# A spectral layer followed by two feed-forward stages on one core: swapping two halves of a result tile with GpSimd copies in place of four DMAs

## The chip, the cores and the metric

The kernel runs on one core of one Trainium2 chip. The metric is the device time in microseconds (us) from one launch, and the figure for a kernel is the median over its runs.

## The reference

The work is a chain of three layers over `x` of shape (4, 3072, 256), in float32.

```python
X = np.fft.rfft(x, axis=1)                       # layer 1: 3072-point spectrum
Yr = Xr @ w_r - Xi @ w_i + b_r                   # complex 256x256 mix of every frequency
Yi = Xr @ w_i + Xi @ w_r + b_i
Y  = sign(Y) * max(abs(Y) - 0.01, 0)             # soft shrink, real and imaginary part
y  = np.fft.irfft(Y, n=3072, axis=1)
xk, xr = mixes of y and y shifted by one token   # layer 2: 256 -> 1024 -> 256, gated
z  = sigmoid(xr @ w_r) * (max(xk @ w_k, 0)**2 @ w_v)
out = (h * tanh(softplus(h))) @ w_out            # layer 3: h = z @ w_in, 256 -> 2048 -> 256
```

## The kernel before

Most products are made of three matmuls in a reduced float32 format: each operand is split into a high part (a ScalarE copy that rounds) and a low part (a VectorE subtraction), and high x high, high x low and low x high are summed in PSUM. The function `split` does this, so its two lines L77 (ScalarE) and L78 (VectorE) stand for many tiles, and tiles are told apart by name.

The transform is a 96 x 32 factorisation. It takes place in the first fifth of the time. The pieces are:

- `s1(b, q)`, the 96-point stage: 32 calls of 8 products, from tiles `xs`/`XS0` of `x` and the table `FC`. The first 12 calls use plain float32. Tiles carry the 96 rows at partitions 16 to 111, and 16 rows of zeros ahead of them are written by GpSimd (`new_x`) and VectorE (`new_F`), so that products run over 112 rows. `s1_ev` copies results out and stores them to device memory.
- a loop over 48 groups `u` (a turn of the loop below), 12 for each of the four batches. A turn issues `s2(u + 1)`, the 32-point stage from a tile `A` that `load_A` fetched and `split_A` split; `s2_ev(u + 1)`, which splits its result from PSUM into `Xh`, `Xl`; `mix(u)`, the complex mix by three real products with tables `WX` (`k1p` is the shared product, `mxp` the two sums, and the bias enters as a product of `SEL` and `BR`); `above(u)` and `shrink(u)`, the soft shrink; and `is1(u - 2)`, the 32-point inverse stage, from `Yh`, `Yl`, which `split_Y(u - 2)` made. `is1_ev(u - 3)` copies the result out of the one PSUM buffer `i1p` into a tile `Cs`, and stores it. In 20 of the turns (2 to 5, and two of every three from 8 to 30) an `s1` is issued as well; the others are called plain turns below.
- from turn 33 on, `early(k)` begins the 96-point inverse stage and layer 2 within the loop.

The result of `mix` has the real and imaginary halves of one group in the same partitions but in an order that the inverse stage can't use. `shrink(u)` therefore writes its result over the tile `yt` (one buffer), and four DMAs on SP's queue copy quarters of it (64 partitions x 256) into a tile `Y` with the halves rearranged. The next `mix` writes `yt` again, and so has to wait for those DMAs.

Engines run their instructions in the order of the code; nothing is reordered. Small steps of the weight preparation for layers 2 and 3 are put between (`bg(2)`, twice a turn): a weight takes 17 steps, eight of which are VectorE instructions on 128x512 elements. After the loop come layer 2 (L886, L924 and others) and layer 3 (L1140, L1188, L1189).

Of the kernel before, what the change touches and what calls it, by code (L numbers as in the profile page):

```python
# [8 lines left out]
F32 = mybir.dt.float32  # L9
# [4 lines left out]
ALU = mybir.AluOpType  # L14
# [15 lines left out]
def kernel(  # L30
# [129 lines left out]
    ps1p = ps1.__enter__()  # L160

    FC = p1sp.tile([128, N2, 2, N1], F32R, name="FC")
    PAD = 16
    KR, XR = slice(0, PAD + N1), slice(PAD, PAD + N1)
    MC = p1p.tile([128, 2, 2, 192], F32R, name="MC")
    WC = p1p.tile([128, 2, 2, 128], F32R, name="WC")
    WX = p1p.tile([128, 2, 3, 2, D], F32R, name="WX")
# [6 lines left out]
    def new_F(q):  # L174
        tag, n = ((("dec_v", 1), ("dec_b", 1)) + (("Cs", 2),) * 2 + (("A", 4),) * 4)[q]
        Ft[q] = p1p.tile([128, 512], F32, tag=tag, name="ctmp", bufs=n)
        nc.vector.memset(Ft[q][0:PAD, 0:384], 0.0)

    def load_F(q):
        for c in (slice(0, 192), slice(192, 384)) if q == 0 else (slice(0, 384),):  # L180
            nc.sync.dma_start(out=Ft[q][XR, c], in_=c_f[:, q * 384 + c.start:q * 384 + c.stop])
            yield

    def split_F(q):
        v = Ft[q][KR, 0:384].rearrange("p (n c) -> p n c", n=4)
        split(v, FC[KR, 4 * q:4 * q + 4, 0, :], FC[KR, 4 * q:4 * q + 4, 1, :])

    cst = {}

# [40 lines left out]
        split(v, WX[:, :, c, 0, :], WX[:, :, c, 1, :])  # L230

    def load_bias():
        t = cst["b"] = p1p.tile([128, 2, D], F32, tag="T", name="bias", bufs=2)
        nc.gpsimd.memset(t, 0.0)
        for p, n in ((0, 1), (32, 1), (64, 2), (96, 2)):
            for k in range(n):
                nc.sync.dma_start(out=t[p:p + 1, k, :], in_=b_r.partition_broadcast(1))
        for p in (0, 32):
            nc.sync.dma_start(out=t[p:p + 1, 1, :], in_=b_i.partition_broadcast(1))

    def make_bias():
        t = cst["b"]
        nc.scalar.copy(out=BR, in_=t)
        for p in (32, 96):
            nc.vector.tensor_tensor(out=BR[p:p + 1], in0=t[p:p + 1], in1=BR[p:p + 1], op=ALU.subtract)

    def make_sel():
        t = p1p.tile([128, 512], F32, tag="T", name="sel", bufs=2)
        s, z = t[:, 0:256].rearrange("p (k n) -> p k n", k=2), t[:, 256:512]
        nc.gpsimd.memset(t, 0.0)  # L250
        for p in (0, 32):
            nc.gpsimd.memset(s[p:p + 1], 1.0)
            nc.gpsimd.memset(s[p:p + 1, 1, 96:97], 0.0)
# [30 lines left out]

    def new_x(b, q):
        t = xs_t[b, q] = p1sp.tile([128, 4, D], F32, tag="xs", name="xs", bufs=3) if b else XS0[q // 4][:, q % 4]
        nc.gpsimd.memset(t[0:PAD], 0.0)

    def x_loads(b, q):
        xv = x[b].rearrange("(p n) d -> p n d", n=N2)[:, 4 * q:4 * q + 4, :]  # L290
        for c in (slice(0, 2), slice(2, 4)) if b + q == 0 else (slice(0, 4),):
            nc.sync.dma_start(out=xs_t[b, q][XR, c], in_=xv[:, c, :])
            yield

    def load_x(b, q):
        new_x(b, q)
        for _ in x_loads(b, q):
            pass

    def split_x(b, q):  # L300
        t = xs_t.pop((b, q))
        h = p1sp.tile([128, 4, D], F32R, tag="xh", name="xh", bufs=3)
        l = p1sp.tile([128, 4, D], F32R, tag="xl", name="xl", bufs=3)
        split(t[KR], h[KR], l[KR])
        xh_t[b, q] = (h, l)

    def warm(n):
# [8 lines left out]
    def s1(b, q):  # L316
        i = 8 * b + q
        plain = i < NAT
        if plain:
            h = xs_t.pop((b, q))  # L320
            f = Ft[q][:, 0:384].rearrange("p (n c) -> p n c", n=4)
        else:
            h, l = xh_t.pop((b, q))
        if b == 0:
            st = XS0[q // 4][0:N1, q % 4]
        elif i < 11:
            st = pkp.tile([N1, 4, D], F32, tag=("D", "Dh", "Dl")[q], name="st", bufs=1)
        else:
            st = p1sp.tile([N1, 4, D], F32, tag="st", name="st", bufs=2)
        for e in range(2):  # L330
            p = ps1p.tile([N1, 2, D], F32, tag=("s1" if i >= NAT or e == 0 else "mx"), name="s1p")
            for m in range(2):
                n2 = 4 * q + 2 * e + m
                if plain:
                    nc.tensor.matmul(
                        out=p[:, m, :], lhsT=f[KR, 2 * e + m, :], rhs=h[KR, 2 * e + m, :], start=True, stop=True
                    )
                    continue
                for k, (w, v) in enumerate(((0, h), (0, l), (1, h))):
                    nc.tensor.matmul(  # L340
                        out=p[:, m, :], lhsT=FC[KR, n2, w, :], rhs=v[KR, 2 * e + m, :],
                        start=(k == 0), stop=(k == 2),
                    )
            s1_t.append((b, q, e, st, p))

    def s1_ev():
        b, q, e, st, p = s1_t.popleft()
        if e == 1 or 8 * b + q >= NAT:
            nc.scalar.copy(out=st[:, 2 * e:2 * e + 2, :], in_=p)
        else:  # L350
            nc.vector.tensor_copy(out=st[:, 0:2, :], in_=p)
# [11 lines left out]
    def store_kept(q):  # L363
        nc.sync.dma_start(out=scr1[1][:, 4 * q:4 * q + 4, :], in_=kept.pop(q))
# [93 lines left out]

    def shrink(u):
        t, up = mx_t.pop(u)  # L460
        nc.vector.scalar_tensor_tensor(out=t, in0=t, scalar=LAM, in1=up, op0=ALU.add, op1=ALU.min)
        y = Y_t[u] = p1p.tile([128, 2, D], F32, tag="T", name="Y", bufs=2)
        for e in range(2):
            for c in range(2):
                nc.sync.dma_start(out=y[64 * c:64 * c + 64, e, :], in_=t[64 * e:64 * e + 64, c, :])

    def split_Y(u):
        yh = p1p.tile([128, 2, D], F32R, tag="Yh", name="Yh", bufs=2)
# [267 lines left out]
    for u in range(NU + 3):  # L736
        if 0 < u < NU - 1:
            s2(u + 1)
        if s1_t:
            s1_ev()  # L740

        def fill():
            if 2 <= u < NU + 2:
                split_Y(u - 2)
            while s1_t:
                s1_ev()
            if u > 2:
# [36 lines left out]
        if u > U_E:
            early(u - U_E - 1)
# [538 lines left out]
```

## Time and profile before

| | |
|---|---|
| median of 3 runs | 2070.87 us (2067.3 to 2074.36) |
| the profiled execution | 2071.17 us, of which its span is 2069.4 us |
| TensorE busy | 1991.1 us, 96% of the span |
| VectorE busy | 1515.1 us, 73% |
| ScalarE busy | 1172.2 us, 57% |
| GpSimd busy | 57.2 us, 3% |

TensorE's busy time is a mean over stages that differ. Below, a stretch is named by its bounds in us from the span's start. The loop's turns are counted by the VectorE instruction at L451, which makes the sum of `mix`: turn 0's starts at 55.59, turn 1's at 62.28, turn 32's at 283.83 and turn 47's, the last, at 379.49.

### The profile page before, as it was taken

The page shows a single profiled execution, that of the slowest core. Times are in us where ns is not written, and L with a number is a line of the kernel's source. Part 1 is how long each engine was busy: PE and PEld are TensorE (multiplying, and loading weights), DVE is VectorE, ACT ScalarE, POOL GpSimd, SP SyncE. Part 2 cuts the span into 40 slices and gives each one's busy share as a digit, 9 for nine tenths or more (in the row PEclk, how much of TensorE's full clock was granted, in tenths as well). Part 3 has the DMA queues.
Part 4 walks back from the last instruction along what each step waited for, and adds up shares of the span by engine and source line. Part 5 has one row for each costly group of instructions (what it writes and reads, how often), then busy time and mean ns, then how long its engine had stood idle before and what let it go on. Part 6 is the DMA issues. An engine that isn't in the chain of part 4 may idle for free.

```text
span 2069.4 us, 33457 instructions
## 1 busy us (share of the span) xinstructions
PE 1991.1 (96%) x13026; PEld 1886.1 (91%) x13026; DVE 1515.1 (73%) x2451; ACT 1172.2 (57%) x1793; POOL 57.2 (3%) x77
## 2 busy tenths in 40 slices
PE   7888888899999999999999999999999999999999
PEld 5777777799999999999989999999999999999998
DVE  5677777577777677777558877778777877778785
ACT  3566655677777777777654444444444444444444
POOL 3100000000000000000000000000000000000000
PEclk8999989899999999999999999999999999999999
DMA  8676755321212121212010000100010100100000
GB/s 258 175 199 195 203 154 143 92 65 49 75 47 75 49 65 57 67 58 65 16 46 22 30 23 21 32 24 29 21 32 21 30 23 21 32 24 29 22 11 21
DMA packets 87117, 135.64 MB, mean 66 GB/s; under 512 B 9448, under 2 KB 63952, under 8 KB 86960
## 3 DMA queue, kind: packets, MB, share of 16 engines
q1 hardware_dynamic: 83376, 120.93, 20.4%
q0 software_dynamic: 3584, 12.58, 1.6%
q8 instruction: 103, 1.69, 0.4%
q14 instruction: 54, 0.44, 0.1%
HBM read 70.56 MB, written 50.33 MB: 58 GB/s over the span
## 4 chain that ended last, share of the span: by engine, by line
PE 81%; ACT 0%; DVE 0%; issue 0%; ACTq 0%
PE h L1140 19%; PE o L1188 17%; PE kp L886 13%; PE vp L924 13%; PE o L1189 9%; PE pp L863 3%; PE p L1140 3%; PE pp L562 3%; PE hp L829 1%; PE h0p L829 0%; PE i1p L480 0%; PE s1p L562 0%; PE pp L536 0%; ACT Yh L77 0%; ACT Cs L492 0%; DVE ob L1204 0%
## 5 line engine op out<-in xcount | busy, mean ns | idle before, releaser
L1188 PE MATMUL o<-WO,gh 128*128 128x512 f32 x1536 | 562.0, 394 | 0.0
L1189 PE MATMUL o<-WO,gl 128*128 128x256 f32 x1536 | 430.3, 280 | 0.0
L1140 PE MATMUL h<-xS,WS 128*128 128x256 f32 x2208 | 350.9, 281 | 0.0
L1153 ACT COPY p1s<-p 128x256 f32<-128x256 f32 x184 | 68.5, 372 | 471.9 <-PE p L1140 470.9
L1188 PEld LDWEIGHTS o<-WO,gh 128*128 128x128 f32 x1536 | 288.9, 188 | 43.3
L1140 PEld LDWEIGHTS h<-xS,WS 128*128 128x128 f32 x2208 | 299.6, 188 | 16.1
L886 PE MATMUL kp<-xk,WK 128*128 128x384 f32 x1536 | 292.2, 338 | 0.0
L1189 PEld LDWEIGHTS o<-WO,gl 128*128 128x128 f32 x1536 | 289.5, 188 | 0.2
L924 PE MATMUL vp<-kh,WV 128*128 128x384 f32 x1024 | 281.2, 336 | 0.0
L886 PEld LDWEIGHTS kp<-xk,WK 128*128 128x128 f32 x1536 | 268.9, 189 | 0.3
L1143 DVE TENSOR_TENSOR C<-h,p1s 128x512 f32<-128x512 f32 x184 | 127.2, 691 | 158.3 <-PE h L1140 156.3
L911 DVE TENSOR_TENSOR kl<-kr,kh 128x768 fp32r<-128x768 f32 x128 | 122.9, 960 | 162.3 <-ACT kr L910 160.9
L1125 DVE TENSOR_TENSOR gl<-g,gh 128x1024 fp32r<-128x1024 f32 x184 | 223.7, 1216 | 2.1 <-ACT g L1122 2.1
L1121 ACT ACTIVATE gh<-C 128x1024 fp32r<-128x1024 f32 x184 | 195.7, 1064 | 10.8 <-DVE C L1143 10.7
L1122 ACT ACTIVATE g<-C 128x1024 f32<-128x1024 f32 x184 | 193.1, 1050 | 0.0
L1140 PE MATMUL h<-xS,WI 128*128 128x256 f32 x1104 | 189.8, 280 | 0.0
L1143 DVE TENSOR_TENSOR C<-h,wu 128x512 f32<-128x512 f32 x368 | 187.7, 552 | 0.3 <-PE h L1140 0.3
L924 PEld LDWEIGHTS vp<-kh,WV 128*128 128x128 f32 x1024 | 186.2, 188 | 0.0
L924 PE MATMUL vp<-kl,WV 128*128 128x384 f32 x512 | 171.5, 335 | 0.0
L909 ACT ACTIVATE kh<-kr 128x768 fp32r<-128x768 f32 x128 | 108.3, 846 | 89.3 <-PE vp L924 89.1
L1140 PEld LDWEIGHTS h<-xS,WI 128*128 128x128 f32 x1104 | 155.7, 188 | 0.0
L1143 DVE TENSOR_TENSOR wu<-h,C 128x512 f32<-128x512 f32 x184 | 126.6, 688 | 34.9 <-PE h L1140 31.1
(187 smaller groups left out, 3143.1 us busy)
## 6 DMA issues: line engine op xcount, KB each, us to landing
Y<-yt SPq DMA_DIRECT2D x192, 64.0 KB
scr<-Cs SPq DMA_DIRECT2D x48, 256.0 KB
D<-scr SPq DMA_DIRECT2D x32, 384.0 KB
x2d<-r POOLq DMA_DIRECT2D x32, 384.0 KB, 3.5
x<-x2d SPq DMA_DIRECT2D x24, 512.0 KB
out_dram<-ob SPq DMA_DIRECT2D x96, 128.0 KB
A<-scr SPq DMA_DIRECT2D x44, 256.0 KB
xs<-in_x_dram SPq DMA_DIRECT2D x24, 384.0 KB
```

The lines of the kernel that those rows point to most:

```text
L886: nc.tensor.matmul(out=p[:, m, 0:TA], lhsT=WK[:, dh, w, f * 128:(f + 1) * 128], rhs=hl[:, v, dh, :], start=(i == 0), stop=(i == 5),)
L909: nc.scalar.activation(out=kh, in_=kr, func=AF.Square)
L911: nc.vector.tensor_tensor(out=kl, in0=kr, in1=kh, op=ALU.subtract)
L924: nc.tensor.matmul(out=p[:, o, 0:TA], lhsT=WV[:, f, w, o * 128:(o + 1) * 128], rhs=v[:, m, :], start=(f == 0 and i == 0), stop=(f == 7 and ...
L1121: nc.scalar.activation(out=gh, in_=c, func=AF.Mish)
L1122: nc.scalar.activation(out=g, in_=c, func=AF.Mish)
L1125: nc.vector.tensor_tensor(out=gl, in0=g, in1=gh, op=ALU.subtract)
L1140: nc.tensor.matmul(out=out, lhsT=a(l), rhs=xS[:, v, b, :], start=(n == 0), stop=(n == 2))
L1143: nc.vector.tensor_tensor(out=out, in0=x0, in1=x1, op=ALU.add)
L1153: nc.scalar.copy(out=p1s, in_=p1)
L1188: nc.tensor.matmul(out=o[m], lhsT=gh[:, m2, ms], rhs=WO[:, f], start=(f == 0), stop=False)
L1189: nc.tensor.matmul(out=o[m][:, 0, :], lhsT=gl[:, m2, ms], rhs=WO[:, f, 0, :], start=False, stop=(f == 15))
```

## The change

Five things change. The shrink writes straight into `Y`, and three GpSimd copies of 64 x 256 rearrange it in place, through a small tile `sw` that takes its place in the one-buffer ring `K1`, which the ScalarE copy `K` of `mix` uses too. `split_A` stands a turn later. `is1_ev` stands at the head of a turn rather than behind `split_A`. Zero rows are gone: tiles hold 96 rows at partitions 0 to 95. Ahead of the loop, the mix tables and the bias are loaded and prepared sooner, and the bias is spread over the rows that need it by GpSimd copies instead of six DMAs.

```diff
     def load_bias():
-        t = cst["b"] = p1p.tile([128, 2, D], F32, tag="T", name="bias", bufs=2)
+        t = cst["b"] = p1p.tile([128, 2, D], F32, tag="Yl", name="bias", bufs=2)
         nc.gpsimd.memset(t, 0.0)
-        for p, n in ((0, 1), (32, 1), (64, 2), (96, 2)):
-            for k in range(n):
-                nc.sync.dma_start(out=t[p:p + 1, k, :], in_=b_r.partition_broadcast(1))
-        for p in (0, 32):
-            nc.sync.dma_start(out=t[p:p + 1, 1, :], in_=b_i.partition_broadcast(1))
+        nc.sync.dma_start(out=t[0:1, 0, :], in_=b_r.partition_broadcast(1))
+        nc.sync.dma_start(out=t[0:1, 1, :], in_=b_i.partition_broadcast(1))
 
     def make_bias():
         t = cst["b"]
+        nc.gpsimd.tensor_copy(out=t[32:33], in_=t[0:1])
+        for p in (64, 96):
+            for k in range(2):
+                nc.gpsimd.tensor_copy(out=t[p:p + 1, k, :], in_=t[0:1, 0, :])
         nc.scalar.copy(out=BR, in_=t)
         for p in (32, 96):
-            nc.vector.tensor_tensor(out=BR[p:p + 1], in0=t[p:p + 1], in1=BR[p:p + 1], op=ALU.subtract)
+            nc.gpsimd.tensor_tensor(out=BR[p:p + 1], in0=t[p:p + 1], in1=BR[p:p + 1], op=ALU.subtract)
...
     def new_x(b, q):
         t = xs_t[b, q] = p1sp.tile([128, 4, D], F32, tag="xs", name="xs", bufs=3) if b else XS0[q // 4][:, q % 4]
-        nc.gpsimd.memset(t[0:PAD], 0.0)
...
     def shrink(u):
         t, up = mx_t.pop(u)
-        nc.vector.scalar_tensor_tensor(out=t, in0=t, scalar=LAM, in1=up, op0=ALU.add, op1=ALU.min)
         y = Y_t[u] = p1p.tile([128, 2, D], F32, tag="T", name="Y", bufs=2)
-        for e in range(2):
-            for c in range(2):
-                nc.sync.dma_start(out=y[64 * c:64 * c + 64, e, :], in_=t[64 * e:64 * e + 64, c, :])
+        nc.vector.scalar_tensor_tensor(out=y, in0=t, scalar=LAM, in1=up, op0=ALU.add, op1=ALU.min)
+        w = p1p.tile([128, D], F32, tag="K1", name="sw", bufs=1)[0:64]
+        nc.gpsimd.tensor_copy(out=w, in_=y[64:128, 0, :])
+        nc.gpsimd.tensor_copy(out=y[64:128, 0, :], in_=y[0:64, 1, :])
+        nc.gpsimd.tensor_copy(out=y[0:64, 1, :], in_=w)
...
+    load_consts()
+    load_bias()
+    load_A(2)
     load_x(1, 3)
-    load_A(2)
     s1(1, 2)
...
     s2(0)
-    s1(1, 3)
+    split_mix(0)
     s2_ev(0)
     split_A(1)
+    split_mix(2)
+    split_mix(1)
+    make_bias()
+    s1(1, 3)
...
     s2_ev(1)
-    split_mix(0)
-    make_bias()
-    split_mix(2)
-    split_mix(1)
     load_A(4)
...
     for u in range(NU + 3):
         if 0 < u < NU - 1:
             s2(u + 1)
+        if u > 2:
+            is1_ev(u - 3)
         if s1_t:
             s1_ev()
...
-        if u + 4 < NU:
-            split_A(u + 4)
-        if u > 2:
-            is1_ev(u - 3)
+        if 0 < u < NU - 3:
+            split_A(u + 3)
```

The order of the instructions on an engine shows what this moves. First ScalarE (ACT) in the loop, from turn 10's `K` to turn 11's, as it was; `K` is the copy of the shared product, `yc` belongs to the shrink, and a name in brackets is the engine or DMA whose semaphore the instruction waits for.

```order
L449 COPY K_1294<-k1p 128x256 [waits PE_49,Activation_49]
L456 ACTIVATE yc<-yt 128x512 [waits DVE_49]
L77 CAST Xh<-s2p 128x768 [waits PE_49]
L77 CAST Yh<-Y 128x512 [waits DMAHW4_49,DMAHW5_49,DMAHW3_49,DMAHW2_49]
L77 CAST Ah<-A 128x512 [waits DMAHW7_49]
L492 COPY Cs<-i1p 128x512 [waits DMAHW0_49]
L449 COPY K_1365<-k1p 128x256 [waits PE_49,Activation_49]
```

And the same stretch of the changed kernel.

```order
L446 COPY K_1260<-k1p 128x256 [waits PE_49,Activation_49,Pool_49]
L453 ACTIVATE yc<-yt 128x512 [waits DVE_49]
L490 COPY Cs<-i1p 128x512 [waits DMAHW4_49,PE_49]
L77 CAST Xh<-s2p 128x768 [waits PE_49]
L77 CAST Yh<-Y 128x512
L77 CAST Ah<-A 128x512 [waits DMAHW6_49]
L446 COPY K_1331<-k1p 128x256 [waits PE_49,Activation_49,Pool_49]
```

`Cs` has moved from fifth place behind `yc` to the first, `Yh` waits for no DMA any more, and `K` has a new wait for GpSimd (Pool). On GpSimd itself the loop before holds only the zero rows (one instruction in each turn with an `s1`); now these are the rows of two turns.

```order
L461 COPY sw<-Y 64x256 [waits DVE_49]
L462 COPY Y<-Y 64x256 [waits Pool_49]
L463 COPY Y<-sw 64x256 [waits Pool_49]
L461 COPY sw<-Y 64x256 [waits DVE_49]
L462 COPY Y<-Y 64x256 [waits Pool_49]
L463 COPY Y<-sw 64x256 [waits Pool_49]
```

The three copies run one after another, each waiting for the one ahead. The third place is the DMA queue of SP ahead of the loop, before the change: `yt` and `yc` are the buffers that the mix weights are loaded into, and `A`, `xs`, `st` and `XS` are the tiles named above.

```order
L378 DMA A<-scr1a 128x2x256 x2
L292 DMA xs<-in_x_dram 96x1024
L378 DMA A<-scr1a 128x2x256
L367 DMA scr_0_57<-XS_82 64x1024 x2
L200 DMA yt<-in_w_r_dram 128x2x256
L200 DMA yc<-in_w_i_dram 128x2x256
L292 DMA xs<-in_x_dram 96x1024
L378 DMA A<-scr1a 128x2x256
L237 DMA bias<-in_b_r_dram 1x256 x6
L239 DMA bias<-in_b_i_dram 1x256 x2
L364 DMA scr_1_58<-st 96x1024
```

And with the change.

```order
L375 DMA A<-scr1a 128x2x256 x2
L197 DMA yt<-in_w_r_dram 128x2x256
L197 DMA yc<-in_w_i_dram 128x2x256
L232 DMA bias<-in_b_r_dram 1x256
L233 DMA bias<-in_b_i_dram 1x256
L375 DMA A<-scr1a 128x2x256
L289 DMA xs<-in_x_dram 96x1024
L364 DMA scr_0_57<-XS_82 64x1024 x2
L289 DMA xs<-in_x_dram 96x1024
L375 DMA A<-scr1a 128x2x256
L361 DMA scr_1_58<-st 96x1024
```

The weights and the bias have moved ahead of one `A` and one `xs` load, and six DMAs are gone from in front of the store. TensorE's instructions stand in the same order in both kernels.

## Rows read from the trace of the kernel before

**Rows 1.** Busy time by stretch; the columns name themselves, PEclk is the granted clock

```profile
62.28:283.83 221.55, 182.05 (x1298) 168.59 (x1297) 157.50 (x230) 139.11 (x263) 15.06 (x15) 0.96 0.68 191
283.83:379.49 95.66, 78.43 (x539) 71.62 (x537) 68.53 (x113) 52.31 (x105) 0.00 (x0) 0.94 0.53 143
379.49:389.22 9.73, 4.75 (x14) 3.99 (x15) 5.49 (x17) 4.38 (x13) 0.00 (x0) 0.54 0.31 89
389.22:2069.40 1680.18, 1676.13 (x10981) 1604.19 (x10979) 1251.86 (x2036) 951.96 (x1367) 24.58 (x33) 1.00 0.12 38
```

**Rows 2.** Waits from 62.28 to 389.22: who waited for whom, total, times, longest

```profile
PE i1p L480 <- ACT Cs L492: 55.5, 32, 5.2
DVE yt L451 <- DMA Y<-yt: 50.0, 37, 4.6
...
ACT Ah L77 <- DMA A<-scr: 10.8, 10, 2.8
```

**Rows 3.** Timeline of turn 43, a plain turn: start, duration, instruction, wait

```profile
355.19 0.69 DVE L451 TENSOR_TENSOR yt<-mxp,K 128x512 f32<-128x512 f32 x1 [1.01 <-DMA Y<-yt]
...
356.58 0.69 DVE L461 SCALAR_TENSOR_TENSOR yt<-yt,yc 128x512 f32<-128x512 f32 x1 [0.70 <-ACT yc L456]
...
357.30 2.38 SPq L465 DMA_DIRECT2D Y<-yt  x4
...
359.81 0.37 ACT L449 COPY K<-k1p 128x256 f32<-128x256 f32 x1
...
361.22 0.69 DVE L451 TENSOR_TENSOR yt<-mxp,K 128x512 f32<-128x512 f32 x1 [0.28 <-DMA Y<-yt]
```

**Rows 4.** TensorE's timeline at full clock: parts of two turns with an s1

```profile
63.28 0.28 PE L340 MATMUL s1p<-xh,FC 112*96 112x256 f32 x1
...
64.58 0.28 PE L340 MATMUL s1p<-xh,FC 112*96 112x256 f32 x1
...
72.96 0.50 PE L480 MATMUL i1p<-Yh,WC 128*128 128x512 f32 x1
...
73.76 0.36 PE L396 MATMUL s2p<-MC,Ah 128*128 128x192 f32 x2
...
77.48 0.28 PE L340 MATMUL s1p<-xh,FC 112*96 112x256 f32 x1
```

**Rows 5.** VectorE's groups from 62.28 to 283.83: busy us, mean ns, idle before

```profile
L78 DVE TENSOR_TENSOR xl<-xs,xh 112x1024 fp32r<-112x1024 f32 x18 | 21.9, 1216 | 0.0
...
L137 DVE SCALAR_TENSOR_TENSOR dec_v<-dec_b,dec_v 128x512 f32<-128x512 int32 x7 | 4.9, 693 | 0.2
...
L126 DVE TENSOR_SCALAR dec_b<-dec_v 128x512 int32<-128x512 int32 x7 | 3.0, 427 | 0.2
```

**Rows 6.** GpSimd's groups of the whole span, by shape

```profile
L78 POOL TENSOR_TENSOR x2h<-x,x2h 128x1024 fp32r<-128x1024 f32 x1 | 2.4, 2396 | 9.8 <-PE vp L924 9.8
L252 POOL MEMSET sel<- 1x256 f32 x2 | 0.6, 304 | 0.1
```

**Rows 7.** Timeline late in layer 2: GpSimd's one subtraction and VectorE beside it

```profile
1027.26 0.96 DVE L911 TENSOR_TENSOR kl<-kr,kh 128x768 fp32r<-128x768 f32 x1 [0.66 <-ACT kr L910]
...
1031.07 1.19 DVE L911 TENSOR_TENSOR kl<-kr,kh 128x768 fp32r<-128x768 f32 x1 [2.25 <-ACT kr L910]
...
1029.05 2.40 POOL L78 TENSOR_TENSOR x2h<-x,x2h 128x1024 fp32r<-128x1024 f32 x1 [9.79 <-PE vp L924]
```

**Rows 8.** Timeline ahead of the loop: SP's queue, ScalarE, VectorE

```profile
35.99 4.80 SPq L237 DMA_DIRECT2D bias<-in_b_r_dram  x6
...
48.09 2.85 SPq L378 DMA_DIRECT2D A<-scr  x2
...
54.33 0.62 ACT L77 CAST Ah<-A 128x512 fp32r<-128x512 f32 x1 [3.07 <-DMA A<-scr]
...
55.59 0.68 DVE L451 TENSOR_TENSOR yt<-mxp,K 128x512 f32<-128x512 f32 x1
```

**Rows 9.** TensorE's timeline behind the last turn

```profile
383.01 0.80 PE L480 MATMUL i1p<-Yh,WC 128*128 128x512 f32 x1 [5.20 <-ACT Cs L492]
```

More of the change, by code (lines that the diff above doesn't have):

```diff
@@ L162 @@
     FC = p1sp.tile([128, N2, 2, N1], F32R, name="FC")
-    PAD = 16
-    KR, XR = slice(0, PAD + N1), slice(PAD, PAD + N1)
     MC = p1p.tile([128, 2, 2, 192], F32R, name="MC")
@@ L176, in new_F @@
         Ft[q] = p1p.tile([128, 512], F32, tag=tag, name="ctmp", bufs=n)
-        nc.vector.memset(Ft[q][0:PAD, 0:384], 0.0)
     def load_F(q):
         for c in (slice(0, 192), slice(192, 384)) if q == 0 else (slice(0, 384),):
-            nc.sync.dma_start(out=Ft[q][XR, c], in_=c_f[:, q * 384 + c.start:q * 384 + c.stop])
+            nc.sync.dma_start(out=Ft[q][0:N1, c], in_=c_f[:, q * 384 + c.start:q * 384 + c.stop])
             yield
     def split_F(q):
-        v = Ft[q][KR, 0:384].rearrange("p (n c) -> p n c", n=4)
-        split(v, FC[KR, 4 * q:4 * q + 4, 0, :], FC[KR, 4 * q:4 * q + 4, 1, :])
+        v = Ft[q][0:N1, 0:384].rearrange("p (n c) -> p n c", n=4)
+        split(v, FC[0:N1, 4 * q:4 * q + 4, 0, :], FC[0:N1, 4 * q:4 * q + 4, 1, :])
     cst = {}
@@ L232, in load_bias @@
     def load_bias():
-        t = cst["b"] = p1p.tile([128, 2, D], F32, tag="T", name="bias", bufs=2)
+        t = cst["b"] = p1p.tile([128, 2, D], F32, tag="Yl", name="bias", bufs=2)
         nc.gpsimd.memset(t, 0.0)
-        for p, n in ((0, 1), (32, 1), (64, 2), (96, 2)):
-            for k in range(n):
-                nc.sync.dma_start(out=t[p:p + 1, k, :], in_=b_r.partition_broadcast(1))
-        for p in (0, 32):
-            nc.sync.dma_start(out=t[p:p + 1, 1, :], in_=b_i.partition_broadcast(1))
+        nc.sync.dma_start(out=t[0:1, 0, :], in_=b_r.partition_broadcast(1))
+        nc.sync.dma_start(out=t[0:1, 1, :], in_=b_i.partition_broadcast(1))
     def make_bias():
         t = cst["b"]
+        nc.gpsimd.tensor_copy(out=t[32:33], in_=t[0:1])
+        for p in (64, 96):
+            for k in range(2):
+                nc.gpsimd.tensor_copy(out=t[p:p + 1, k, :], in_=t[0:1, 0, :])
         nc.scalar.copy(out=BR, in_=t)
         for p in (32, 96):
-            nc.vector.tensor_tensor(out=BR[p:p + 1], in0=t[p:p + 1], in1=BR[p:p + 1], op=ALU.subtract)
+            nc.gpsimd.tensor_tensor(out=BR[p:p + 1], in0=t[p:p + 1], in1=BR[p:p + 1], op=ALU.subtract)
     def make_sel():
-        t = p1p.tile([128, 512], F32, tag="T", name="sel", bufs=2)
+        t = p1p.tile([128, 512], F32, tag="Yh", name="sel", bufs=2)
         s, z = t[:, 0:256].rearrange("p (k n) -> p k n", k=2), t[:, 256:512]
@@ L291, in x_loads @@
         for c in (slice(0, 2), slice(2, 4)) if b + q == 0 else (slice(0, 4),):
-            nc.sync.dma_start(out=xs_t[b, q][XR, c], in_=xv[:, c, :])
+            nc.sync.dma_start(out=xs_t[b, q][0:N1, c], in_=xv[:, c, :])
             yield
@@ L303, in split_x @@
         l = p1sp.tile([128, 4, D], F32R, tag="xl", name="xl", bufs=3)
-        split(t[KR], h[KR], l[KR])
+        split(t[0:N1], h[0:N1], l[0:N1])
         xh_t[b, q] = (h, l)
@@ L335, in s1 @@
                     nc.tensor.matmul(
-                        out=p[:, m, :], lhsT=f[KR, 2 * e + m, :], rhs=h[KR, 2 * e + m, :], start=True, stop=True
+                        out=p[:, m, :], lhsT=f[0:N1, 2 * e + m, :], rhs=h[0:N1, 2 * e + m, :], start=True, stop=True
                     )
@@ L340, in s1 @@
                     nc.tensor.matmul(
-                        out=p[:, m, :], lhsT=FC[KR, n2, w, :], rhs=v[KR, 2 * e + m, :],
+                        out=p[:, m, :], lhsT=FC[0:N1, n2, w, :], rhs=v[0:N1, 2 * e + m, :],
                         start=(k == 0), stop=(k == 2),
@@ L645 @@
     store_rest(5)
-    load_consts()
     load_x(1, 4)
     load_A(3)
-    load_bias()
     make_sel()
     s2(0)
-    s1(1, 3)
+    split_mix(0)
     s2_ev(0)
     split_A(1)
+    split_mix(2)
+    split_mix(1)
+    make_bias()
+    s1(1, 3)
     store_kept(0)
```

## The prediction

> **What bounds the kernel now.** I read the table of busy time by stretch first. From 389.22 us to the end TensorE is busy for 1676.13 of 1680.18 us at a granted clock of 1.00 [rows 1]. The change touches nothing there, and no wait taken from another engine could shorten it. All that can move lies in the first 389 us, which is the start up to turn 0, the loop and its tail. In the two stretches of the loop TensorE is busy for 182.05 of 221.55 us and 78.43 of 95.66 us, VectorE for 157.50 and 68.53, and the granted clock averages 0.96 and 0.94 [rows 1], so some of TensorE's busy time is at 1.2 GHz instead of 2.4. No engine is full here; a chain of waits sets the pace.
>
> The list of waits names it. TensorE waits 55.5 us in front of the inverse stage for `Cs`, the copy that empties its one PSUM buffer, and VectorE waits 50.0 us, in 37 of 47 turns, for the DMAs that read `yt` [rows 2]. The timeline of a plain turn shows how these are one chain. The sum `yt` starts at 355.19, the shrink ends at 357.27, four DMAs are then issued over 2.38 us, and the next `yt` starts at 361.22, let go by the DMA although `K` was ready at 360.18 [rows 3]. So a turn is 6.03 us, of which 3.95 us is the handover through DMA. ScalarE stands in `yc` until `yt` comes, and `Cs` is queued behind it; that is the wait of TensorE.
>
> **The change, part by part.** *Handover.* The four DMAs go, and `yt` is free once the shrink has read it. In place of them the next `K` waits for the third copy. The new chain of a turn is 2.08 us from `yt` to the end of the shrink, three copies of c us with a hop of about 0.06 us each, `K` at 0.37 us [rows 3], and two hops of some 0.05 us: 2.73 + 3c. No copy of GpSimd is in the trace. From below there is its memset of 256 elements, which is 304 ns; from above its subtraction, 2396 ns for 1024 elements or 2.34 ns each, which gives 0.60 us for 256, and 0.70 with a start-up cost [rows 6]. A copy has one input where the subtraction has two, so it is nearer to the memset; I take c = 0.40 us. Turns by this chain are then 3.93 us, and 3.64 to 4.83 at the bounds. That is below what TensorE needs, so the handover stops being the bound and the engines' own work is next.
>
> The Trainium skill ("GPSIMD Engine Reference", section 3.1) has about 1 cycle per element for an operation bound by one port and 2.6 for one with two inputs; as an estimate from that page a copy would be about 0.31 us with the memset's start-up, and the chain 3.7 us.
>
> *TensorE's own work.* At full clock the 32-point stage and the mix take 3.72 us (73.76 to 77.48), the inverse stage 0.80 (72.96 to 73.76), and an `s1` 1.42 (eleven spacings in 63.28 to 64.58, times 12/11) [rows 4]. A plain turn needs 4.52 us and one with an `s1` 5.94. *VectorE's own work.* Its 157.50 us over 31 turns hold 21.9 us of `xl` [rows 1, 5]. A weight costs five instructions of about 0.69 us and three of about 0.42 [rows 5], 4.7 us in 17 steps at four a turn, so 1.1 a turn. Without both, a turn needs 135.6 / 31 - 1.1 = 3.27 us, and one with an `s1` 4.49. The weight's eight instructions fall into about two of every 4.25 turns, which need 2.36 us more: 5.63 plain, 6.85 with an `s1`. In these VectorE is the bound; in the others TensorE is. The mean is 0.47 x 6.85 + 0.53 x 5.94 = 6.37 us with an `s1`, and 0.47 x 5.63 + 0.53 x 4.52 = 5.04 plain.
>
> *GpSimd beside VectorE.* A VectorE subtraction with both operands in SBUF took 1.19 us instead of 0.96 when it started at 1031.07, while GpSimd's subtraction ran until 1031.45 [rows 7]: 0.23 us lost in 0.38 of overlap, or 0.6 of it. The copies start behind the shrink, and take 3 x 0.46 = 1.4 us; the next on VectorE is `Xl`, one of whose operands is in PSUM, for about 0.9 us, and then `Yl` with two in SBUF. If only `Yl` is hit, a turn loses about 0.6 x 0.4 = 0.2 us where VectorE is the bound, 0.1 on average. From below the loss is nothing; from above all 1.4 us of copying is lost in every turn.
>
> The Trainium skill ("SBUF — State Buffer", section "Who interferes with whom") says that a VectorE instruction with two SBUF inputs contends with a GpSimd instruction that reads SBUF, and that the loser is blocked fully rather than slowed. By that rule the loss is the whole overlap, 0.4 us in place of 0.2, which over 46 turns adds some 5 us to the sum; the row has 0.6 of the overlap, so it agrees on the collision but not on its size. It speaks against the change, and is the first rival below.
>
> *Sum of the loop.* Turns 1 to 32: 20 x 6.47 + 11 x 5.14 = 186 us, against 221.55 before [rows 1]: -36. Turns 32 to 47 are plain but carry the first parts of layer 2, some 4 us of TensorE; I take 5.14 + 0.26 = 5.4 us, 81 against 95.66 [rows 1]: -15. The limits from below are TensorE's 168.5 and 72 us.
>
> *`is1_ev` first, `split_A` later.* Moving `Cs` up takes `Xh`, `Yh` and `Ah` from in front of it, which would otherwise still hold TensorE back once the DMA wait is gone. Its own store is the same DMA, now ahead of the store of `st` and the load of `A` on SP's queue; each is one issue of about half a us that no one waits for. `Ah` now waits a turn less early for its load. Of the 10.8 us of waits for `A` and the few for other loads [rows 2] I leave half to come back on a path: +7 us.
>
> *Start.* On SP eight bias issues become two; six took 4.80 us [rows 8]. The loads of `A` behind them, issued at 48.09, held ScalarE until 54.33, and turn 0's sum was at 55.59 [rows 8]. The `Ah` that waited is a turn later now, and the tables are cast while ScalarE waits for the 96-point stage anyway. Against that one `xs` load stands behind 0.5 MB of weights and comes about 2 us later. I take -4 us; the bounds are 0 and -7. *Tail.* TensorE waits 5.20 us for `Cs` at 383.01, behind the last DMA handover [rows 9]; with a handover of 1.4 us instead of 4 and `Cs` at the head, -4 us of the 9.73.
>
> *Zero rows.* 32 GpSimd memsets and eight of VectorE go; GpSimd is busy for 15.06 of 221.55 us [rows 1] and nothing waits for it in the loop. Fewer rows don't shorten a product: 31 of the 32-point stage and the mix, over 128 rows, take 0.120 us each, and those of `s1`, over 112, 0.118 [rows 4]; so 96 rows are 0, and so are the six tiny copies of the bias, hidden behind the wait for the next `A`.
>
> Total: -36 - 15 + 7 - 4 - 4 = -52 us. The profiled execution took 2071.17 us, 0.3 above the median, so 2071 - 52 gives about **2019 us**.
>
> **Rivals.** (1) *Blocked VectorE.* If VectorE loses all 1.4 us of copying, it needs 1.3 more than my sum allows in 46 turns: +60 us, or 2079 at worst and about 2060 where half falls into idle time. `Xl` with its PSUM operand and TensorE's bound in half the turns speak against it. (2) *Another wait behind the first.* Loads of `A`, stores and the k1p and st hand-ons follow closely, and turns shorten by half as much: 2071 - 27 = 2044. The 10.8 us for `A` speaks for it; the DMA share of 0.68 [rows 1], of which the four copies go, against. (3) *Slower: slow copies.* `K` waits for the third copy, and everything on ScalarE behind `K`. The turn is 2.73 + 3c; the loop becomes longer than before when this passes (221.55 + 95.66 + 8) / 46 = 7.07 us, at c = 1.45 us. At c = 1.6 it is 7.53 x 46 - 317 - 8 = +21, or 2092. The copies cross partitions, which no row shows; but c would have to be 2.4 times the two-input rate. (4) *No effect:* TensorE waits as long elsewhere, for `Yl` or the Xh split: 2071. (5) *Better overlap:* TensorE is full in most turns and the bunches of weight steps even out: 168.5 + 72 in the loop, -53 - 23 - 8, or 1987 to 2002.
>
> **How the numbers follow.** My forecast, 2002 to 2035, has 0.66; better overlap 0.07; another wait (2035 to 2058) 0.12; blocked VectorE (2045 to 2079) 0.07; no effect 0.04; slow copies 0.04. A measurement of this kernel can tell about 0.3%, or 6 us, from no change. Faster by more holds the forecast, the better overlap, the other wait and half of the blocked case: 0.89. Within 0.3%: 0.06. Slower: 0.05. The range of 2000 to 2046 leaves out the tail of the better overlap and most of (1), (3) and (4), about 0.2.
>
> **What would show it.** Right: no wait of `yt` for a DMA; turns of about 5.1 and 6.4 us between L448's; copies near 0.4 us; `K` hardly waiting for GpSimd; TensorE's wait for `Cs` below 10 us; a clock near 1.00 in the loop; the last stretch still 1680 us. Wrong: copies above 0.8 us, a wait of `K` for GpSimd in most turns, `Yl` and `Al` well above 0.69 us, or waits for `A` that grow.

## The result and the profile after

The changed kernel takes 2005.9 us (median; 2004.53 to 2008.91 in 4 runs) against 2069.09 of the kernel before, run on the same chip. The ratio is 0.9693, with a 95% interval of 0.9669 to 0.9717: about 63 us less, where 52 were predicted. Its profiled span is 2005.3 us against 2069.4.

First the busy time by stretch, cut at the same marks as [rows 1]: turns 0, 1, 32 and 47 start at 47.91, 52.94, 232.31 and 315.58 (the sum is now L448), and the first product of layer 2 at 325.98.

```profile
47.91:52.94 5.03, 3.88 (x31) 3.46 (x29) 3.88 (x7) 2.21 (x4) 1.93 (x3) 1.00 1.06 262
52.94:232.31 179.37, 171.66 (x1308) 161.46 (x1309) 159.12 (x230) 139.29 (x263) 42.85 (x93) 1.00 0.64 189
232.31:315.58 83.27, 74.47 (x535) 67.91 (x534) 69.45 (x116) 52.98 (x106) 25.47 (x45) 0.98 0.37 115
315.58:325.98 10.40, 5.95 (x20) 4.20 (x20) 5.48 (x17) 4.39 (x13) 1.19 (x3) 0.66 0.15 51
325.98:2005.30 1679.32, 1675.44 (x10981) 1603.50 (x10979) 1251.89 (x2036) 952.29 (x1367) 24.50 (x33) 1.00 0.12 38
```

TensorE is now busy for 171.66 of 179.37 us in turns 1 to 32, that is 96% where it was 82%, at a clock of 1.00. The next to last row is the tail, from the sum of turn 47 to layer 2: no shorter than before, and at a low clock (0.66; it was 0.54). The last row is what nothing touches.

| stretch | before | after | difference | predicted |
|---|---|---|---|---|
| up to turn 1 | 62.28 | 52.94 | -9.3 | -4 |
| turns 1 to 32 | 221.55 | 179.37 | -42.2 | -36 |
| turns 32 to 47 | 95.66 | 83.27 | -12.4 | -15 |
| waits for `A` left over, in the loop | | | none in the list | +7 |
| tail, up to the first product of layer 2 | 9.73 | 10.40 | +0.7 | -4 |
| layers 2 and 3 | 1680.18 | 1679.32 | -0.9 | 0 |
| sum | | | -64.1 | -52 |

The list of waits from 52.94 to 325 answers to [rows 2].

```profile
ACT yc L453 <- DVE yt L448: 51.1, 36, 2.6
PEld i1p L478 <- DVE Yl L78: 18.4, 27, 1.5
ACT K L446 <- POOL Y L463: 16.3, 21, 2.0
...
PE i1p L478 <- DVE Yl L78: 10.1, 15, 1.2
...
PE i1p L478 <- ACT Yh L77: 9.1, 8, 3.0
DVE Al L78 <- ACT Ah L77: 4.1, 8, 0.6
```

The 55.5 us of TensorE for `Cs`, the 50.0 of `yt` for DMAs and the 10.8 for loads of `A` are all gone. TensorE's largest waits, for `Yl` and `Yh`, sum to 19 us, and `K` waits for GpSimd in 21 turns. The handover itself, in the timeline of the last two turns (it answers to [rows 3]):

```profile
311.29 0.68 DVE L448 TENSOR_TENSOR yt<-mxp,K 128x512 f32<-128x512 f32 x1
...
312.67 0.69 DVE L459 SCALAR_TENSOR_TENSOR Y<-yt,yc 128x512 f32<-128x512 f32 x1 [0.70 <-ACT yc L453]
...
313.43 0.40 POOL L461 COPY sw<-Y 64x256 f32<-64x256 f32 x1 [2.66 <-DVE Y L459]
...
313.73 0.69 DVE L78 TENSOR_TENSOR Yl<-Y,Yh 128x512 fp32r<-128x512 f32 x1 [0.37 <-ACT Yh L77]
...
313.89 0.80 POOL L462 COPY Y<-Y 64x256 f32<-64x256 f32 x1
...
314.75 0.39 POOL L463 COPY Y<-sw 64x256 f32<-64x256 f32 x1
...
315.17 0.37 ACT L446 COPY K<-k1p 128x256 f32<-128x256 f32 x1 [1.54 <-POOL Y L463]
...
315.58 0.69 DVE L448 TENSOR_TENSOR yt<-mxp,K 128x512 f32<-128x512 f32 x1 [1.15 <-ACT K L446]
```

From one sum to the next it is 4.29 us, all of it this chain: 2.07 to the end of the shrink, 1.78 for the copies, then `K`. An undisturbed copy takes 0.39 to 0.40 us; the second began while `Yl` was running and took 0.80. GpSimd's groups by shape, over the whole span, for [rows 6]:

```profile
L463 POOL COPY Y<-sw 64x256 f32<-64x256 f32 x48 | 26.6, 553 | 3.0
L462 POOL COPY Y<-Y 64x256 f32<-64x256 f32 x48 | 22.8, 474 | 3.0
L461 POOL COPY sw<-Y 64x256 f32<-64x256 f32 x48 | 22.1, 461 | 197.2 <-DVE Y L459 193.7 <-DVE yp L543 3.5
```

The three means sum to 1.49 us a turn, 0.50 a copy. VectorE in turns 1 to 32, first before the change (for `xl` see [rows 5]):

```profile
L78 DVE TENSOR_TENSOR Al<-A,Ah 128x512 fp32r<-128x512 f32 x31 | 21.3, 688 | 10.7 <-ACT Ah L77 10.7
...
L78 DVE TENSOR_TENSOR Yl<-Y,Yh 128x512 fp32r<-128x512 f32 x31 | 21.1, 682 | 0.0
```

and then beside the copies:

```profile
L78 DVE TENSOR_TENSOR Al<-A,Ah 128x512 fp32r<-128x512 f32 x31 | 22.1, 714 | 3.7 <-ACT Ah L77 3.5
L78 DVE TENSOR_TENSOR xl<-xs,xh 96x1024 fp32r<-96x1024 f32 x18 | 21.9, 1216 | 1.4 <-ACT xh L77 1.4
...
L78 DVE TENSOR_TENSOR Yl<-Y,Yh 128x512 fp32r<-128x512 f32 x31 | 21.4, 691 | 0.0
```

The start, as the timeline of SP's queue, ScalarE and VectorE shows it (against [rows 8]):

```profile
43.79 2.23 SPq L375 DMA_DIRECT2D A<-scr  x2
...
46.22 0.37 ACT L446 COPY K<-k1p 128x256 f32<-128x256 f32 x1
...
47.91 0.67 DVE L448 TENSOR_TENSOR yt<-mxp,K 128x512 f32<-128x512 f32 x1
```

`K` of turn 0 is not held by any `Ah` now. And the tail, ScalarE and TensorE behind turn 47 (against [rows 9]):

```profile
317.73 0.32 ACT L573 COPY ya<-s1p 128x192 f32<-128x192 f32 x1
317.94 0.59 ACT L490 COPY Cs<-i1p 128x512 f32<-128x512 f32 x1
...
318.42 0.63 ACT L77 CAST Yh<-Y 128x512 fp32r<-128x512 f32 x1
...
319.10 0.80 PE L478 MATMUL i1p<-Yh,WC 128*128 128x512 f32 x1 [2.99 <-ACT Yh L77]
...
323.55 0.63 ACT L77 CAST Yh<-Y 128x512 fp32r<-128x512 f32 x1
...
324.23 0.80 PE L478 MATMUL i1p<-Yh,WC 128*128 128x512 f32 x1 [1.46 <-ACT Yh L77]
```

The `Y` of turn 46 was complete at 315.14, but its `Yh` starts at 318.42, behind `yc`, layer 2's `yT` and `ya` copies, and `Cs`. From turn 47's sum to this product it is 3.52 us (315.58 to 319.10), as it was before (379.49 to 383.01 [rows 9]).

### The profile page after: what moved, and what is told of

It is laid out like the page before. It is cut to its first block, busy times and chain, and to the rows that moved or that the text cites. A ratio compares the mean times of both kernels' runs of the same rounds, so it can differ in the third digit from the quotient of the medians.

```text
span 2005.3 us, 33189 instructions
## 1 busy us (share of the span) xinstructions
PE 1968.8 (98%) x13026; PEld 1867.8 (93%) x13026; DVE 1513.3 (75%) x2441; ACT 1172.7 (58%) x1793; POOL 103.2 (5%) x196
## 4 chain that ended last, share of the span: by engine, by line
PE 84%; ACT 0%; DVE 0%; issue 0%; ACTq 0%
PE h L1138 20%; PE o L1186 18%; PE kp L884 14%; PE vp L922 13%; PE o L1187 9%; PE pp L861 3%; PE p L1138 3%; PE pp L560 3%; PE hp L827 1%; PE h0p L827 0%; PE i1p L478 0%; PE s1p L560 0%; PE pp L534 0%; ACT Yh L77 0%; ACT Cs L490 0%; DVE ob L1202 0%
## 5 line engine op out<-in xcount | busy, mean ns | idle before, releaser
L1123 DVE TENSOR_TENSOR gl<-g,gh 128x1024 fp32r<-128x1024 f32 x184 | 223.8, 1216 | 2.1 <-ACT g L1120 2.1
L1119 ACT ACTIVATE gh<-C 128x1024 fp32r<-128x1024 f32 x184 | 195.6, 1063 | 10.9 <-DVE C L1141 10.8
```

The costliest lines, as they stand in the source:

```text
L1119: nc.scalar.activation(out=gh, in_=c, func=AF.Mish)
L1123: nc.vector.tensor_tensor(out=gl, in0=g, in1=gh, op=ALU.subtract)
```

## The experiments

**Theory:** the DMA handover was the pace of the loop, and everything else in the change is worth something only once it is gone, the start apart. **Rivals:** the order on ScalarE (`Cs` first) is what freed TensorE; or the copies are the new bound, so that less copying would bring more.

*1. The handover alone, in the kernel before.*

```diff
-        nc.vector.scalar_tensor_tensor(out=t, in0=t, scalar=LAM, ...)
+        nc.vector.scalar_tensor_tensor(out=y, in0=t, scalar=LAM, ...)
-        for e in range(2): for c in range(2): nc.sync.dma_start(...)
+        three nc.gpsimd.tensor_copy through sw, as in the change
```

> The kernel before with nothing changed but the shrink: three GpSimd copies in place of the four DMAs. My theory, that the handover through DMA sets the pace of the turns and all else follows: yt waits for no DMA, but Cs still stands behind Ah on ScalarE, so TensorE keeps part of its wait for Cs, 55.5 us before; 20 to 45 us faster, 2025 to 2050. Rival, that the order on ScalarE is what the loop gains by (Cs at the head of a turn): at most 10 us faster, TensorE's wait for Cs still above 45 us. Rival, that the gain is from the start and the zero rows: no change.

Measured: 2018.19 us, ratio 0.9761 (0.9745 to 0.9777), -50 us; turns 1 to 32 take 183.49 us and 32 to 47 85.71. It is below what I expected. Its list of waits, from turn 1 to the first product of layer 2 as in [rows 2]:

```profile
PE i1p L481 <- ACT Cs L493: 21.6, 20, 3.5
...
ACT K L449 <- POOL Y L466: 11.8, 18, 1.5
```

TensorE's wait for `Cs` fell from 55.5 to 21.6 us with `Cs` in its old place: most of it was the DMA wait seen from further down the chain.

*2. All but the handover.* The changed kernel with its four DMAs back.

```diff
-        three nc.gpsimd.tensor_copy through sw
+        for e in range(2): for c in range(2): nc.sync.dma_start(...)
```

> The changed kernel with the four DMAs back in the shrink. My theory: plain turns are at 6.0 us again and the loop is as long as before; what is left is the start, some 9 us, so about 2060 (2053 to 2066). Rival of the order on ScalarE: 2015 to 2035, since Cs and split_A stand as in the changed kernel. Rival of the start and the zero rows: 2006, as the changed kernel.

Measured: 2063.34 us, 0.9972 (0.9963 to 0.9981); turns 1 to 32 take 220.14 us, 32 to 47 97.66. The waits, within the same marks:

```profile
DVE yt L448 <- DMA Y<-yt: 54.5, 37, 5.1
...
PE i1p L477 <- ACT Yh L77: 29.5, 22, 5.0
```

With `Cs` at the head TensorE's wait has changed its name to `Yh`, and the loop is as long as it was.

*3. The order alone, in the kernel before.*

```diff
+        if u > 2: is1_ev(u - 3)          # at the head of the turn
-        if u + 4 < NU: split_A(u + 4)
-        if u > 2: is1_ev(u - 3)
+        if 0 < u < NU - 3: split_A(u + 3)
```

> The kernel before with is1_ev at the head of a turn and split_A a turn later, and nothing else. My theory: the DMA handover still sets the pace, so 0 to 6 us faster, 2063 to 2069; TensorE's wait moves from Cs to other places. Rival of the order: 30 to 50 us faster, 2019 to 2039.

Measured: 2070.22 us, 1.0008 (0.9998 to 1.0017). Nothing, and a little above what I expected: turns 1 to 32 take 223.56 us.

*4. The handover and the order, in the kernel before* (the edits of 1 and 3).

> The kernel before with the GpSimd copies and the order of the loop, but the start, the bias and the zero rows as before. My theory: the whole gain of the loop, about 54 us, so 2012 to 2019; turn 1 starts near 62 us as before, and the start is worth the 9 us that are missing. Rival of the zero rows, which take 15 us of GpSimd's time in the loop and stand ahead of its copies in turns with an s1: the copies wait for them, K waits for the copies, and 5 to 15 us of the loop's gain are lost, 2020 to 2030.

Measured: 2009.84 us, 0.9721 (0.9707 to 0.9736). That is below what I expected. The order that was worth nothing by itself is worth 8 us on top of the handover.

*5. `Cs` back behind `split_A`, in the changed kernel.*

```diff
-        if u > 2: is1_ev(u - 3)          # at the head of the turn
         if 0 < u < NU - 3: split_A(u + 3)
+        if u > 2: is1_ev(u - 3)
```

> The changed kernel with is1_ev moved back behind split_A; split_A stays a turn later. It tells which of the two moves gave the 8 us between the handover alone and the handover with the order. My theory, that Cs at the head keeps TensorE from waiting for it: TensorE's wait for Cs comes back at 10 us or more, 4 to 8 us slower than the changed kernel, 2010 to 2014. Rival, that split_A's later place is all of it, by turn 0's earlier start: no change, 2004 to 2008.

Measured: 2007.94 us, 0.9706 (0.9691 to 0.972). The wait came back, and the time hardly did; it lies in the rival's range and not in mine:

```profile
PE i1p L478 <- ACT Cs L490: 21.0, 20, 3.0
```

So `Cs` first is worth 0 to 3 us; the intervals overlap. The stretches show both sides of it: with `Cs` back turns 1 to 32 take 182.23 us, 2.9 more, and the tail 8.60, 1.8 less.

*6. `split_A` a turn later, with the handover, in the kernel before; `Cs` stays behind it.*

```diff
-        if u + 4 < NU: split_A(u + 4)
+        if 0 < u < NU - 3: split_A(u + 3)
```

> The kernel before with the GpSimd copies and with split_A a turn later; the copy Cs stays where it was, behind split_A. With the copies alone the time was 2018.2 us, with the copies and both moves of the order 2009.8. If the order's 8 us are mostly split_A's later place, as the small effect of moving Cs back says: 2010 to 2012, with turns 1 to 32 at 180 to 183 us. The rival, that the two moves pay only together, because Cs stands behind the split and both wait: 2014 to 2018.

Measured: 2012.69 us, and as a ratio 0.9721 (0.9708 to 0.9734), the same as with `Cs` moved too; the median is 2.9 us above that of run 4. The later split carries most of the order's gain, or all of it. Where it acts first is seen on ScalarE ahead of turn 0; in the kernel with the handover alone:

```profile
52.13 0.62 ACT L77 CAST Ah<-A 128x512 fp32r<-128x512 f32 x1 [3.19 <-DMA A<-scr]
52.65 0.37 ACT L449 COPY K<-k1p 128x256 f32<-128x256 f32 x1
```

and with the later split:

```profile
49.90 0.61 ACT L77 CAST Ah<-A 128x512 fp32r<-128x512 f32 x1
50.42 0.36 ACT L449 COPY K<-k1p 128x256 f32<-128x256 f32 x1
```

The `Ah` that waited 3.19 us for its load stood in front of `K`; turn 1 starts at 56.42 instead of 58.06. The rest lies mostly in the last turns: 82.80 us from turn 32 to 47 against 85.71.

*7. The start alone*: the changed kernel with the DMAs and the old order of the loop back (the edits of 2 and 3 undone).

> The changed kernel with the four DMAs back and the loop's order as it was: only the start (and the zero rows, worth nothing) is changed. The loop with the DMA handover took about 317 us wherever it stood, so only turn 1 can move, and the later end with it. If the start is worth what the difference of two other runs says (2063.3 with it and the order, 2070.2 with the order alone): 2062 to 2066, with turn 1 at 55 to 58 us against 62.28. The rival, that the earlier start comes from the later split and the order alone: 2068 to 2071, with turn 1 at 60 to 62.

Measured: 2063.97 us, 0.9976 (0.9967 to 0.9985), -5.7 us; turn 1 starts at 58.21 instead of 62.28. The loads and tables are worth their part with either handover.

*8. The zero rows back, in the changed kernel* (16 rows ahead of the 96, with their memsets, and products over 112 rows).

```diff
+        nc.gpsimd.memset(t[0:PAD], 0.0)
-                        out=p[:, m, :], lhsT=f[0:N1, ...], rhs=h[0:N1, ...]
+                        out=p[:, m, :], lhsT=f[KR, ...], rhs=h[KR, ...]
```

> The changed kernel with the 16 zero rows back, written by GpSimd and VectorE as before, and products over 112 rows. My prediction gave the rows nothing: 2003 to 2010, no difference that can be told. Rival, that 15 us of GpSimd in the loop stand ahead of its copies, or that 96 rows start sooner in the first 50 us: 4 to 12 us slower than the changed kernel.

Measured: 2005.99 us, 0.9693 (0.9677 to 0.971). Worth nothing.

*9. `sw` in the spent tile `yc` instead of the ring that `K` uses, in the changed kernel.*

```diff
-        w = p1p.tile([128, D], F32, tag="K1", name="sw", bufs=1)[0:64]
+        w = up[0:64, 0, :]
```

> The changed kernel with the small tile of the copies in the spent tile yc instead of the ring that K uses, so that yc, 1.1 us later in the turn, waits for the third copy and K waits for none. Theory that K's 16.3 us of waits for GpSimd are on the path of the plain turns: they go, and turns 32 to 47 shorten from 83.3 to 77 to 80 us; 3 to 8 us faster than the changed kernel, 1998 to 2003. Rival, that TensorE and VectorE are the bound there anyway (74.5 and 69.5 of 83.3 us busy): the waits only move to other places, 2004 to 2008.

Measured: 2006.41 us, 0.9695 (0.968 to 0.9709). The 16.3 us that `K` waited for GpSimd are gone from the list, and this row stands in their place (51.1 in the changed kernel):

```profile
ACT yc L453 <- DVE yt L448: 68.9, 44, 2.9
```

For most turns the wait only moved along ScalarE, and the time stayed. It was on the path at the ends of the loop: turn 0 takes 3.80 us instead of 5.03 and turn 46 3.34 instead of 4.29. Against that turns 1 to 32 take 181.09 us, 1.7 more; why is not shown.

*10. Twice the copies, in the changed kernel*: the first is made four times, so six in a turn.

```diff
         nc.gpsimd.tensor_copy(out=w, in_=y[64:128, 0, :])
+        nc.gpsimd.tensor_copy(out=w, in_=y[64:128, 0, :])    # three more
```

> The changed kernel with the first of the three copies made four times, so six copies a turn, the added ones reading SBUF as the others do. By the chain 2.73 + copies, with copies of 0.40 to 0.55 us, the handover grows by 1.4 us to about 5.5 us a turn: plain turns rise to 5.5 or more, turns with an s1 hardly; the wait of K for GpSimd goes from 16 to 50 us or more, and the time to 2018 to 2035. Rival, that GpSimd's reading costs by blocking VectorE: VectorE's busy time in the loop rises by 10 us or more, and its Yl and Al get longer than 0.75 us on average.

Measured: 2057.56 us, 0.9946 (0.9931 to 0.996): 51.6 us more than three copies, and well above my range. The six means sum to 3.33 us, so 1.84 us more of copying, and three more hops, cost 1.1 us a turn. The waits from turn 1 to the first product of layer 2, and VectorE's `Al`:

```profile
ACT K L446 <- POOL Y L466: 95.3, 46, 3.4
DVE yt L448 <- ACT K L446: 42.2, 39, 2.5
```

```profile
L78 DVE TENSOR_TENSOR Al<-A,Ah 128x512 fp32r<-128x512 f32 x43 | 35.9, 834 | 4.0 <-ACT Ah L77 3.9
```

Here `K` waits for the last copy in all 46 turns of the list: the chain is 2.73 + 0.18 + 3.33 = 6.24 us, and 6.56 us (98.40 over 15) is what turns 32 to 47 take. Of the 2.02 us more of chain 1.1 showed, so three copies leave about 0.9 us a turn, on the mean, before that point. The rival's sign came too, in part: VectorE's busy time in turns 1 to 47 is 241.53 us, 13 more than with three copies, and `Al` is above 0.75 us, though `Yl` at 0.71 is not. How much of the 51.6 us that makes is not shown. The DMAs are gone in this kernel as well, so it is the length of the handover that costs, and not only the DMAs' traffic.

*11. The tail: `Cs` and the split of `Y` ahead of layer 2's first copies, in the changed kernel.*

```diff
+        if u in (NU - 1, NU):            # behind shrink(u), ahead of early()
+            is1_ev(u - 2)
+            split_Y(u - 1)
```

The same steps are left out of turns 48 and 49, where they stood.

> The changed kernel, and at the end of the loop ScalarE's copy Cs of turns 45 and 46 and the split of Y of turns 46 and 47 stand ahead of the first copies of layer 2 instead of behind them. If the tail's 9.3 us stay because Yh is queued behind those copies: the inverse stage's first product behind turn 47 starts about 1.5 us sooner, the last one 1.5 to 3 us, and the time is 2003 to 2004.5. The rival, that layer 2's copies only move behind and its first product starts as late: 2005 to 2007, with the first product of layer 2 again about 10.4 us after the start of turn 47's sum.

Measured: 2001.94 us (2000.46 to 2004.16), 0.9673 (0.9659 to 0.9686). Its tail as a stretch, and as TensorE's and ScalarE's timeline:

```profile
315.82:322.24 6.42, 3.70 (x20) 2.49 (x19) 4.24 (x16) 4.29 (x13) 1.59 (x3) 1.00 0.25 83
```

```profile
317.55 0.62 ACT L77 CAST Yh<-Y 128x512 fp32r<-128x512 f32 x1
...
318.22 0.50 PE L478 MATMUL i1p<-Yh,WC 128*128 128x512 f32 x1 [1.88 <-ACT Yh L77]
...
322.24 2.09 PE L887 MATMUL kp<-xk,WK 128*128 128x384 f32 x11
```

The tail takes 6.42 us instead of 10.40, and its clock is 1.00. The kernel is 4 us faster than the changed one by the medians, as the 3.98 us of the tail say; the two ratios' intervals still overlap, so it is the trace that carries this reading.

## Why the prediction was right, and where its sizes were off

*The bound was named rightly.* Undone by itself, the handover takes back all but 5 us (run 2), and alone it gives 50 (run 1). The sum of terms 2.73 + 3c held too: with the three copies of turn 46 it is 2.73 + 1.59 = 4.32, and 4.29 was seen. An undisturbed copy has the 0.40 us that I took; the mean is 0.50, because the collisions with VectorE fell mostly on the copies; the estimate of 0.31 us was too low. The hops of 0.06 us, for which I gave no row, came out at 0.06 to 0.07.

*Turns 1 to 32 (-36, measured -42.2).* Two terms were too dear. I charged 0.1 us a turn, 3 us in all, for VectorE beside GpSimd; VectorE's busy time rose by 1.6 us, from 157.50 to 159.12. The other 3 to 5 us are in the mean over weight steps: I let two of 4.25 turns be bound by VectorE at 5.63 and 6.85 us. The longest turns do take 6.99 us, but TensorE is busy 96% of the stretch, so that fewer turns are bound by VectorE than I counted. From sum to sum, the 20 turns with an `s1` take 5.99 us on the mean, hardly more than the 5.94 of TensorE, where I gave 6.47; the 11 plain ones take 5.42, more than my 5.14. The stretch ended 10.9 us above the 168.5 that I gave as TensorE's limit, and TensorE itself needed 171.66. In that much the rival of a better overlap was right; how the weight steps fall was not tried by a run of its own.

*Turns 32 to 47 (-15, measured -12.4).* The gain was oversized by 2.3 us. TensorE was busy for 74.47 us where I gave it 72, and `K`'s wait for GpSimd is on the path at times, as in the chain of 4.29 us above: without it turn 46 is 0.95 us shorter, and the stretch 81.05 us (run 9). Half of that run's 2.2 us is not `K`'s alone, for turn 44, 5.74 us in the changed kernel and 4.71 in run 9, takes 4.66 in run 8 too, where `K` waits as before.

*The waits that I kept (+7).* They did not come: the list has no wait for `A`. Either move alone takes nearly all of them away. With the handover alone (run 1) 0.8 of the 10.8 us is left, and with the later split and the DMAs (runs 2 and 3) the list has none; with neither (run 7) it is 7.2. In these runs the term had no ground: a split a turn later gives the load more time, and I charged for it.

*The start (-4, measured -9.3).* The loads and tables alone moved turn 1 by 4.1 us (run 7), which is the term. What I left out is turn 0: its own handover, since the loop's terms began at turn 1, and the `Ah` of 3.07 us in front of its `K` [rows 8], which I had read and folded into the same -4. The runs give it in steps: turn 1 starts at 62.28 before, at 58.21 with the start (run 7), at 54.93 with the order too (run 2) and at 52.94 with the handover, so 4.1, 3.3 and 2.0 us. The steps are rough. Five kernels with the same code ahead of the loop have turn 0 start anywhere from 46.37 to 48.55, and with the old start the later split moved turn 1 by 1.6 us and not 3.3 (runs 1 and 6).

*The tail (-4, measured +0.7).* This step failed. The wait for `Cs` that I read in [rows 9] did go, but TensorE then waits 2.99 and 1.46 us for `Yh`, which stands on ScalarE behind layer 2's `yT` and `ya`, and behind `Cs`. I asked what released the old wait and not what stood next in ScalarE's order. Nor could the shorter handover help there: the tail is counted from turn 47's sum, and the last handover that this sum waits for lies ahead of it, in the -15. From the sum on, ScalarE has the same steps to do in both kernels, and the product comes 3.52 us behind it in either. Run 11 moves those steps and gets the 4 us.

*The total.* -52 came within 12 us of -64 partly because the misses have both signs: the loop's first part, the kept waits and the start together gained some 18 us more than I gave them, the last turns and the tail some 7 less.

*Zero rows, `Cs` first, the bias copies.* Nothing for the zero rows, as predicted (run 8; the 18 `xl` over 96 partitions still take 1216 ns). The bias takes five small copies and not the six that I counted. `Cs` first I had taken as needed once the DMA wait was gone; it takes a wait of some 20 us off TensorE's list and 0 to 3 us off the time (runs 5 and 6).

*The rivals.* With three copies VectorE was hardly the one blocked: its busy time in turns 1 to 47 rose by 2.5 us, and the copies lost some 15 (144 of them in 71.5 us, where 0.395 each would be 56.9); with six it lost 13 more. `K` waited for GpSimd in 21 turns, more than the "hardly" of my signs. By the mechanism of slow copies run 10 comes close to the time before with a chain of 6.24 us; it was still 11 to 12 us ahead, and if from there each further us of copying costs one in all 46 turns, the break-even lies near a chain of 6.5 us, or c = 1.25 rather than my 1.45. That is an estimate; no run went so far. Another wait behind the first, and no effect, are excluded by the loop's 54.6 us.

## What to carry to other kernels

When an engine's wait is long, follow it back before moving instructions on it: of TensorE's 55.5 us for `Cs`, 34 were a DMA three steps up the chain, and moving `Cs` and the split alone only renamed the wait. Here small on-chip copies by an idle engine beat a DMA round trip (2.2 us from the end of the shrink to the next sum, against 3.95) where the data was needed in the same turn; it pays as long as the new chain stays below what the busiest engine needs, and doubling the copies is a cheap way to see how far below it is. For each wait that a change removes, read which instruction comes next on the engine that was waited for, at the ends of the loop above all.

## What the runs showed of the hardware

*Who began later lost the collisions, mostly.* These rows are from the changed kernel's start, its turn 0 and its turn 4.

```profile
43.44 1.61 DVE L78 TENSOR_TENSOR Al<-A,Ah 128x512 fp32r<-128x512 f32 x1 [0.84 <-ACT Ah L77]
...
50.90 1.14 POOL L462 COPY Y<-Y 64x256 f32<-64x256 f32 x1
51.11 0.68 DVE L78 TENSOR_TENSOR Al<-A,Ah 128x512 fp32r<-128x512 f32 x1
...
72.37 0.40 POOL L463 COPY Y<-sw 64x256 f32<-64x256 f32 x1
...
72.49 0.82 DVE L78 TENSOR_TENSOR Yl<-Y,Yh 128x512 fp32r<-128x512 f32 x1
```

Of the 144 copies 30 took more than 0.42 us. In 28 of them a VectorE instruction with two operands in SBUF was already running when the copy began, like the copy of 0.80 us above, which lost 0.41 of the 0.53 us that it shared with `Yl`. The other way round, VectorE lost where it began while GpSimd was at work: `Yl` at 72.49 lost 0.14 us of 0.28 shared, and `Al` at 43.44 lost 0.93 of the 1.06 that it shared with GpSimd's second one-row subtraction of the bias, which ended at 44.50. In nearly all of these the loss is the time shared less 0.12 to 0.15 us, and so is the 0.23 of 0.38 in [rows 7] that I had read as a share of 0.6. The copy at 50.90 is one of two that don't fit: it began 0.21 us ahead of `Al` and yet lost 0.75 us, and `Al` nothing. `Xl`, which reads one operand from PSUM, lost nothing: 957 ns on the mean in turns 1 to 32, 955 before. An instruction of the weight steps with one operand in SBUF, `dec_b` from `dec_raw`, did lose: 553 ns on the mean in turns 1 to 47, 421 before. The Trainium skill ("SBUF — State Buffer", section "Who interferes with whom") has issue order, and not the kind of operation, decide which of the two is blocked, and calls it an exclusive lock. The 28 copies agree on the order, and the copy at 50.90 does not; the loss is some 0.13 us less than the whole time shared.

*Few partitions make a copy no cheaper.* Of GpSimd's four copies of one row of 256 elements for the bias three took 393 to 394 ns and one 852, and 64 rows of 256 took 390 to 400 undisturbed.

*The granted clock in the tail.* It averages 0.66 in the changed kernel's 10.40 us, so it is at 1.2 GHz and not 2.4 for the greater part. The products behind TensorE's wait of 2.99 us are at the lower level: the 96-point ones take 0.41 us there, and took 0.25 to 0.28 ahead of it. In run 11 it is 1.00, TensorE's longest wait is 1.88 us, and the same products take 0.26 to 0.28. So 4 us there are partly waiting and partly clock: TensorE's busy time is 5.95 and 3.70 us, for 20 products in either.
